# Column stage of a 2048-point transform: factorization 64 x 32 with stacked real and imaginary parts, one PSUM bank and one set of tasks per frequency

## Chip, cores and metric

One core of one Trainium2 chip. Its engines are PE (TensorE, matmuls), DVE (VectorE), ACT (ScalarE) and POOL (GpSimd); SPq is the queue of SyncE, which issues the transfers. An eviction is the copy of a matmul's result out of PSUM (`ps` in the profile lines). The metric is the device time of one launch in microseconds (us), as a median over several launches.

## The reference

```python
def reference(A_x, A_w_r, A_w_i, B_x, B_w_gate, B_w_up, B_w_down):   # all bf16
    x  = A_x                                    # [1, 2048, 640]
    xn = layernorm(x, axis=-1)
    X  = rfft2(xn, axes=(-2, -1)) * (A_w_r + 1j * A_w_i)             # weights [2048, 321]
    ya = irfft2(X, s=(2048, 640))
    yb = ((xn @ B_w_gate) * (xn @ B_w_up)) @ B_w_down                # 640 -> 1536 -> 640
    return x + ya + yb
```

There are two independent branches: a spectral filter and a gated feed-forward layer. The kernel interleaves them, so that the matmuls of one fill the waits of the other.

## The kernel before

The kernel is written as a list of tasks, each with the engines that it may run on, a duration, its reads and writes, and a priority. At build time a greedy planner places the tasks by these durations. That fixes the order of instructions on every engine; semaphore waits are then derived from the dependencies. The planner counts for a transfer:

```python
_DMA_LEAD = 500.0; _DMA_LAT = 1150.0; _DMA_ISSUE = 500.0     # ns
...
def hold(t, *later):        # t may not start before what `later` waits for is there
    for x in later:
        t.deps |= set(d for d in x.deps if d is not t and d not in later)
```

The 2048 rows are transformed as 64 (stage R, before) times 32 (column stage). The column stage runs in 16 steps. Each step holds two frequencies on two groups of 64 partitions, with the real and the imaginary parts in two PSUM banks:

```python
# for t in range(16):           filter rows: 4 transfers per step, four slots
def em_d(c, t=t):               # D: transform along the 640 axis
    for k in range(5):
        n = 128 if k < 4 else 130
        ins = c.e.matmul(psflat[:, bk*512 + k*128: ... + n], v_uq[:, k, t, :], v_fd[:, k*128: k*128 + n], ...)
# eD: two copies PSUM -> bf16 (128 x 512 and 128 x 130)
def em_c(c, t=t, ar=ar):        # C: complex product with the twiddled table, four matmuls
    c.e.matmul(ps[:, bk,     0:_LP], v_tf[:, t, 0, :], a_r, start=True,  stop=False)
    c.e.matmul(ps[:, bk + 1, 0:_LP], v_tf[:, t, 0, :], a_i, start=True,  stop=False)
    c.e.matmul(ps[:, bk,     0:_LP], v_tf[:, t, 1, :], a_i, start=False, stop=True)
    return c.e.matmul(ps[:, bk + 1, 0:_LP], v_tf[:, t, 2, :], a_r, start=False, stop=True)
# WM (DVE): four products of 256 and one of 260 elements with the filter, f32
# CD (DVE), CB (POOL): combine them to a complex product, bf16
# NG (ACT): three negated or copied pieces
def em_ia(c, t=t, ar=ar):       # IA: back along the rows, ten matmuls of 128 columns
    for k in range(5):
        c.e.matmul(dst, l1, v_ti[:, t, 0, :], start=True,  stop=False)
        ins = c.e.matmul(dst, l2, v_ti[:, t, 1, :], start=False, stop=True)
# eIA: one copy of 128 x 640
```

## Time and profile before

| | before |
|---|---|
| time, median of 3 runs | 206.84 us (206.67 to 207.27) |
| span of the profiled run | 204.3 us |
| PE / DVE / ACT / POOL busy | 98% / 87% / 59% / 11% |
| PE work of the column stage (D, C, IA) | 22.2 us |
| PE waits after 80 us | 0.35 us |

"PE work" counts every matmul by the distance from its start to the start of the next one, since a pipelined matmul is recorded with its latency. A "PE wait" is what is left of such a distance over 90 ns after the streaming time of the matmul is taken off (columns / 2.4 + 2.5 ns, which the spacings of 56, 136 and 216 ns for 128, 320 and 512 columns fit). A missing record of a 512-column matmul is put back first: only where the rest is a multiple of 216 ns, and only as many as the trace lacks of the 360. The profile lines are in the prediction below.

### The profile page before, as it was taken

The page shows a single profiled execution, that of the slowest core. Times are in us where ns is not written, and L with a number is a line of the kernel's source. Part 1 is how long each engine was busy: PE and PEld are TensorE (multiplying, and loading weights), DVE is VectorE, ACT ScalarE, POOL GpSimd, SP SyncE. Part 2 cuts the span into 40 slices and gives each one's busy share as a digit, 9 for nine tenths or more (in the row PEclk, how much of TensorE's full clock was granted, in tenths as well). Part 3 has the DMA queues.
Part 4 walks back from the last instruction along what each step waited for, and adds up shares of the span by engine and source line. Part 5 has one row for each costly group of instructions (what it writes and reads, how often), then busy time and mean ns, then how long its engine had stood idle before and what let it go on. Part 6 is the DMA issues. An engine that isn't in the chain of part 4 may idle for free.

```text
span 204.3 us, 4499 instructions
## 1 busy us (share of the span) xinstructions
PE 199.7 (98%) x1681; PEld 137.2 (67%) x1695; DVE 178.7 (87%) x508; ACT 121.4 (59%) x282; POOL 21.8 (11%) x36
## 2 busy tenths in 40 slices
PE   7999999999999999999999999999999999999995
PEld 7998999554545455465777666666777787777774
DVE  3798999999999999949997997818999999999973
ACT  2379998999976577577999899878420222000000
POOL 0000000000000000003655365310000000000000
PEclk9999999999999999999999999999999999999999
DMA  6999993603139460001333343225033122324212
GB/s 179 301 342 383 387 210 15 67 0 64 32 66 242 86 202 0 3 0 27 66 65 60 68 113 65 65 70 158 0 98 113 55 76 83 112 80 111 83 35 62
DMA packets 30740, 21.69 MB, mean 106 GB/s; under 512 B 10752, under 2 KB 29696, under 8 KB 30592
## 3 DMA queue, kind: packets, MB, share of 16 engines
q1 hardware_dynamic: 29920, 21.06, 40.6%
q10 hardware_dynamic: 800, 0.36, 0.6%
q8 instruction: 13, 0.21, 0.4%
q14 instruction: 7, 0.06, 0.1%
HBM read 16.82 MB, written 2.62 MB: 95 GB/s over the span
## 4 chain that ended last, share of the span: by engine, by line
PE 92%; DVE 6%; issue 1%; ACT 1%
PE ps L969 36%; PE ps L1229 26%; PE ps L989 13%; DVE arena L1070 3%; PE ps L747 3%; PE ps L930 2%; PE ps L1146 2%; PE ps L1239 2%; PE ps L1034 2%; PE ps L1117 2%; PE ps L1118 2%; DVE arena L1073 1%; PE ps L1058 1%; PE ps L1055 1%; PE ps L1057 1%; PE ps L1056 1%
## 5 line engine op out<-in xcount | busy, mean ns | idle before, releaser
L719 ACT ACTIVATE arena<-ps 128x512 bf16<-128x512 f32 (+5 forms) x183 | 97.1, 568 | 48.7 <-PE ps L1146 23.4
L969 PE MATMUL ps<-arena 128*128 128x512 bf16 x346 | 80.1, 379 | 0.9 <-DVE arena L1073 0.3
L969 PEld LDWEIGHTS ps<-arena 128*128 128x128 bf16 x360 | 33.9, 98 | 36.5 <-ACT arena L719 0.8
L1229 PE MATMUL ps<-arena 128*128 128x320 bf16 (+2 forms) x396 | 56.7, 295 | 0.0
L1229 PEld LDWEIGHTS ps<-arena 128*128 128x128 bf16 x396 | 38.0, 98 | 13.9
L989 PE MATMUL ps<-arena 128*128 128x128 bf16 (+1 forms) x360 | 28.2, 237 | 0.1
L989 PEld LDWEIGHTS ps<-arena 128*128 128x128 bf16 x360 | 24.9, 98 | 2.5 <-ACT arena L719 0.7
L1070 DVE TENSOR_TENSOR arena<-ps,arena 128x256 f32<-128x256 f32 x64 | 22.6, 414 | 1.4 <-PE ps L1058 1.2
L1005 DVE TENSOR_TENSOR arena<-arena 128x512 bf16<-128x512 bf16 x36 | 15.3, 425 | 9.0 <-ACT arena L719 8.8
L1093 POOL TENSOR_TENSOR arena<-arena 128x256 bf16<-128x256 f32 x16 | 10.3, 644 | 111.5 <-DVE arena L1086 111.5
L1249 DVE TENSOR_TENSOR arena<-ps,arena 128x320 bf16<-128x320 f32 (+2 forms) x33 | 15.3, 473 | 3.8 <-PE ps L1239 3.8
L1094 POOL TENSOR_TENSOR arena<-arena 128x256 bf16<-128x256 f32 x16 | 11.9, 745 | 0.0
L1117 PE MATMUL ps<-arena 128*128 128x128 bf16 x80 | 10.4, 219 | 0.1
L1118 PE MATMUL ps<-arena 128*128 128x128 bf16 x80 | 10.4, 219 | 0.0
L1117 PEld LDWEIGHTS ps<-arena 128*128 128x128 bf16 x80 | 8.7, 111 | 1.7
L1118 PEld LDWEIGHTS ps<-arena 128*128 128x128 bf16 x80 | 8.7, 112 | 1.4
L1239 PE MATMUL ps<-arena 128*128 128x320 bf16 (+2 forms) x33 | 9.1, 295 | 0.0
L883 DVE TENSOR_TENSOR arena<-arena 128x384 f32<-128x384 bf16 x16 | 8.8, 551 | 0.0
L773 ACT ACTIVATE arena<-arena 128x640 bf16<-128x640 bf16 x10 | 8.3, 825 | 0.0
L782 DVE BATCH_NORM_STATS2 arena<-arena 128x6 f32<-128x320 bf16 x12 | 5.4, 481 | 2.8 <-DMA arena<-in_A_x_dram 2.7
L767 ACT ACTIVATE arena<-arena 128x640 bf16<-128x640 bf16 x10 | 7.3, 734 | 0.3 <-DMA arena<-in_A_x_dram 0.2
L1073 DVE TENSOR_TENSOR arena<-ps,arena 128x260 f32<-128x260 f32 x16 | 7.0, 438 | 0.0
(72 smaller groups left out, 235.7 us busy)
## 6 DMA issues: line engine op xcount, KB each, us to landing
arena<-in_A_x_dram SPq DMA_DIRECT2D x20, 160.0 KB, 2.5
out_dram<-arena SPq DMA_DIRECT2D x31, 80.0 KB, 1.6
arena<-c_tf SPq DMA_DIRECT2D x4, 384.0 KB, 11.2
arena<-in_A_w_r_dram SPq DMA_DIRECT2D x32, 40.1 KB, 2.3
arena<-in_A_w_i_dram SPq DMA_DIRECT2D x32, 40.1 KB, 2.3
arena<-in_B_w_gate_dram SPq DMA_DIRECT2D x4, 320.0 KB, 5.4
arena<-in_A_x_dram SPq DMA_DIRECT2D x1, 1280.0 KB, 10.3
arena<-c_ti SPq DMA_DIRECT2D x2, 512.0 KB, 4.9
```

The costliest lines, as they stand in the source:

```text
L719: return c.e.activation(dst, src, _ACTF.Copy)
L969: ins = c.e.matmul(ps[:, bk, :], v_gw[:, w, j, ft, :], v_xt[:, j, rows], start=(j == 0), stop=(j == 4))
L989: ins = c.e.matmul(ps[:, bk, w * n:(w + 1) * n], v_gw[:, w, j, ft, :], v_xt[:, j, rows], start=(j == 0), stop=(j == 4))
L1005: return c.e.tensor_tensor(v_ht[:, ft0, rows], v_gbf[:, rr, 0, :], v_gbf[:, rr, 1, :], _OP.mult)
L1070: c.e.tensor_tensor(v_p[:, ar, w, :, 128 * h:128 * h + 128].rearrange("p c (m k) -> p c m k", k=4), xh.rearrange("p c (m k) -> p c m k", k ...
L1093: c.e.tensor_tensor(v_y[ar][:, 512:768], p01[:, 0:256], p10[:, 0:256], _OP.add)
L1094: return c.e.tensor_tensor(v_y[ar][:, 256:512], p00[:, 0:256], p11[:, 0:256], _OP.subtract)
L1117: c.e.matmul(dst, l1, v_ti[:, t, 0, :], start=True, stop=False)
L1118: ins = c.e.matmul(dst, l2, v_ti[:, t, 1, :], start=False, stop=True)
L1229: ins = c.e.matmul(ps[:, bk, 0:sl3.stop - sl3.start], v_ht[:, ft, a * 128:(a + 1) * 128], v_wd[:, ft, sl3], start=(ft == 7 and px is None) ...
L1239: return c.e.matmul(ps[:, bank_of(own), 0:sl3.stop - sl3.start], v_sm[:, 2, :], v_v[:, a, sl3], start=False, stop=True)
L1249: return c.e.tensor_tensor(v_out[:, a % 2, sl3], ps[:, bk, 0:sl3.stop - sl3.start], v_xr[:, xs, sl3], _OP.add)
```

## The change

The intent is to halve the C matmuls, since PE bounds the kernel, and to give every frequency its own small tasks. The factors become 32 (stage R) and 64 (column stage). Real and imaginary rows of one frequency lie on partitions 0-63 and 64-127, so one matmul with a [[re, im], [-im, re]] table does a whole complex product. In the same way IA's contraction adds up the products with the filter, and the combines (CD, CB) vanish. The main lines, shortened:

```diff
-_R = 32
+_R = 64
-_NW = 4
+_NW = 2                       # slots of filter rows ...
+_WQ = 4                       # ... each now holds four frequencies
 # filter rows: every second step, six transfers (two of 64 partitions from a
 # broadcast source, four of every other partition), with each row fetched twice
-            td = T("D_%d" % t, "pe", 5 * _d_mm(128), em_d, ... bank="pair", cls="a")
+            for w in range(2):           # w: real, imaginary
+                    for k in range(5):
+                        n = 64 if k < 4 else 65
+                        ins = c.e.matmul(ps[:, bk, k * 64:k * 64 + n], v_uq[:, k, t, :], ...)
+                def em_ed(c, td=td, ar=ar, w=w):
+                    for g in range(2):
+                        ins = copy_on(c, v_a[64 * w:64 * w + 64, ar, 324 * g:324 * g + 321],
+                                      ps[64 * g:64 * g + 64, bk, 0:321])
+            for g in range(2):           # one frequency q = 2t + g each
+                    return c.e.matmul(ps[:, bank_of(c.t), 0:_LP], v_tf[:, q, :], v_a[:, ar, 324*g:324*g + _LP], ...)
                 # WM (DVE): two products of 256 and one of 130 elements, written as bf16
+                wm = T("WM_%d" % q, "dve", 895.0, em_wm, reads=[(b_w, slot of the filter rows)], ..., frees=tc)
+                hold(tc, wm)             # so C waits for the filter rows as well
                 # NG: one negation of 256, on POOL, ACT or DVE
+                def em_ns(c, yr=yr, g=g):
+                    c.e.tensor_copy(yg[:, 833:896], yg[:, 1025:1088])
+                    c.e.tensor_copy(yg[:, 961:1024], yg[:, 769:832])
+                    return c.e.tensor_scalar(yg[:, 896:961], yg[:, 1024:1089], -1.0, None, _OP.mult)
+                T("NS_%d" % q, "pool", 700.0, em_ns, ...)
                 # IA: ten matmuls of 64 columns; eIA: one copy of 128 x 320
 # start: 10 groups of warm-up matmuls instead of 12, smaller fill matmuls, first
 #        statistics partly on ACT
 # schedule: other caps, priorities and slacks (retuned)
... (tables, buffers and views cut)
```

## The prediction

> **What bounds the kernel now.** I read the page first (busy shares, slices, chain), then the groups by form, then a table of windows, then single pieces of the chain.
>
> ```profile
> PE 199.7 (98%) x1681; PEld 137.2 (67%) x1695; DVE 178.7 (87%) x508; ACT 121.4 (59%) x282; POOL 21.8 (11%) x36
> ...
> PEclk9999999999999999999999999999999999999999
> ...
> PE 92%; DVE 6%; issue 1%; ACT 1%
> PE ps L969 36%; PE ps L1229 26%; PE ps L989 13%; DVE arena L1070 3%; PE ps L747 3%; PE ps L930 2%; PE ps L1146 2%; PE ps L1239 2%; PE ps L1034 2%; PE ps L1117 2%; PE ps L1118 2%; DVE arena L1073 1%; PE ps L1058 1%; PE ps L1055 1%; PE ps L1057 1%; PE ps L1056 1%
> ```
>
> TensorE (PE) is busy 98% of 204.3 us at full clock, and 92% of the chain that ended last is matmuls. A busy PE need not be at its peak, so I checked that with the spacing of matmuls in the chain: ten 128-column ones in 0.56 us (56 ns each), five 512-column ones in 1.08 us (216 ns), twelve 320-column ones in 1.63 us (136 ns). These are the array's streaming time plus about 2.5 ns, so nothing is left inside the groups either.
>
> The groups by form give the counts of the part that changes, the column stage (D = L1034, C = L1055 to L1058, IA = L1117 and L1118), and the vector work beside it:
>
> ```profile
> L1034 PE MATMUL ps<-arena 128*128 128x128 bf16 x64 | 5.9, 218 | 0.0
> L1058 PE MATMUL ps<-arena 128*128 128x321 bf16 x16 | 4.8, 300 | 0.0
> L1117 PE MATMUL ps<-arena 128*128 128x128 bf16 x80 | 10.4, 219 | 0.1
> L1117 PEld LDWEIGHTS ps<-arena 128*128 128x128 bf16 x80 | 8.7, 111 | 1.7
> L1034 PEld LDWEIGHTS ps<-arena 128*128 128x128 bf16 x80 | 5.6, 97 | 1.4
> L1070 DVE TENSOR_TENSOR arena<-ps,arena 128x256 f32<-128x256 f32 x64 | 22.6, 414 | 1.4 <-PE ps L1058 1.2
> L1094 POOL TENSOR_TENSOR arena<-arena 128x256 bf16<-128x256 f32 x16 | 11.9, 745 | 0.0
> ```
>
> The 219 ns is the latency of one pipelined matmul, not its cost; the cost is the spacing, 56 ns. The weight loads overlap the matmuls.
>
> Windows by stage (us, then PE, PEld, DVE, ACT, POOL busy, clock, DMA):
>
> ```profile
> 28.00:60.00 32.00, 31.84 (x245) 19.50 (x246) 31.17 (x97) 28.99 (x68) 0.00 (x0) 1.00 0.35 49
> 100.00:112.00 12.00, 11.95 (x123) 8.60 (x123) 10.57 (x37) 11.59 (x33) 6.65 (x10) 1.00 0.32 64
> 112.00:125.00 13.00, 12.62 (x115) 8.50 (x117) 12.51 (x42) 11.94 (x35) 6.93 (x10) 1.00 0.39 84
> 145.00:165.00 20.00, 20.00 (x171) 15.10 (x170) 19.63 (x49) 3.47 (x6) 0.00 (x0) 1.00 0.28 80
> ```
>
> In the column stage (about 89 to 137 us) PE stays full because gate/up matmuls (L969) are interleaved as filler, while VectorE (DVE) and ScalarE (ACT) are nearly full as well. So DVE and ACT are a close second there, and DVE is again in the inverse stage, 145 to 185 us.
>
> **The PE ledger.** With those spacings: L969 360 x 216 = 77.7; L989 240 x 56 + 120 x 109 = 26.5; L1229 52.2; L1239 4.4; L930 and L1146 160 x 56 = 8.9; transposes L844 1.1; column stage D 80 x 56 = 4.5, C 64 x 136 = 8.7, IA 160 x 56 = 8.9, together 22.1. Sum 192.9 us (counts from the program, since some records are missing). The other 11.4 us are: 6.1 before the first transpose (the warm-up matmuls L747, 48 of them in 5.30), 1.1 of cold transposes and fill matmuls before the first gate/up matmul at 7.57, some 1.7 of gaps, and 2.4 after the last matmul. A gain must therefore come out of PE work or out of the start; a wait removed elsewhere has at most 1.7 us to give.
>
> **What the Trainium skill says.** "TensorE: Matmul & The Clock Gate", section "Wait — 56ns, not 53.3ns?": spacing N/2.4 + about 2.5 ns when warm, and a floor of about 25 ns however small N is. The trace agrees for 128, 320 and 512 columns; no matmul of 64 columns is in it. The section "Weight-path perf modes — Fast Weight Load (FWL) and DoubleRow" of that page says that a full 128-column bf16 load is read in four parallel chunks. The trace fits: where PE had run dry (9.47 us), the load and its first matmul start within 0.01 us of each other and the second load starts about 15 ns after the first, so I estimate that a contiguous load holds the array for about 14 ns. IA's stride-4 loads take some 16 ns longer (111 ns mean of L1117, which mixes contiguous ones in, against 97 of L1034), so about 31 ns by estimate. "VectorE: DVE Perf Modes", section "Why PSUM operands drop a tier": fp32 from PSUM runs one element per cycle. The trace agrees (256 elements in 414 ns, four in a row at 330 ns each), so writing the products as bf16 makes none of them faster. "GPSIMD Engine Reference", section "4.1 Engine selection": two-input work is about 2x slower there than on VectorE, one-input roughly at line rate. L1094 at 745 ns agrees with the first; no one-input copy on POOL is in the trace.
>
> **The change part by part.**
>
> *C, removed PE work.* Real and imaginary rows are stacked on the contraction side, so a complex product of 128 rows that took four matmuls becomes two products of 64 frequencies-by-sign each in one matmul: 64 x 136 ns = 8.7 us become 32 x 136 = 4.4. **-4.4 us**, all on the bound engine.
>
> *D, more matmuls.* 80 of 128 columns become 160 of 64, each with the full 128-column weights again. At 64/2.4 + 2.5 = 29 ns, the contiguous load (14 ns) hides: 160 x 29 = 4.7 against 4.5. **+0.2.**
>
> *IA, more matmuls.* 160 of 128 columns become 320 of 64. Four fifths have stride-4 weights; the next load can start only when the previous matmul has started, so I take 33 ns for those (31 + about 2) and 29 for the rest: 256 x 33 + 64 x 29 = 10.3 against 8.9. **+1.4.**
>
> PE total of the column stage: 22.1 - 4.4 + 0.2 + 1.4 = 19.3, **-2.8 us**.
>
> *DVE.* Per old step it does 4 x 330 + 370 + two 65-element combines of about 140, together about 2.0 us, x16 = 32 us. After: per frequency two 256-element products and one of 130, about 330 + 330 + 220 = 0.88, x32 = 28 us. The combines vanish, because IA's contraction does the adding. About **-4 us of DVE**, off the path while PE is full.
>
> *ACT.* D's eviction must now move halves between partitions: four copies of 64 x 321 per step. Between 382 ns for 256 and 595 for 512 elements a 321-element copy costs about 436, so 1.75 us per step instead of 0.88 (595 + 283), +14 us in all. IA's eviction becomes 2 x 436 instead of 705, +2.7. The three negate/copy operations (412 + 247 + 246 = 0.9 per step, 14.5 us) move to POOL, or partly to ACT or DVE. ACT stays about even.
>
> *POOL.* From 21.8 us to perhaps 32 x (0.4 to 0.9 for the negation + 0.6 for three short ones) = 32 to 48 us, by estimate from the two-input rows above, in a stage of 48. Near full, but some of the negation may go elsewhere.
>
> *Weights.* The filter rows come in groups of four frequencies, double-buffered, twice the bytes (each row is fetched for its real and imaginary partition). A group is six transfers; before, two issues on the queue took 1.23 us, so six take about 3.7 us plus 2.3 to land, about 6 us, while the other group lasts some 48/8 = 6 us. Tight, but each may run ahead by a group.
>
> *Start.* 40 warm-up matmuls in place of 48: at 107 ns (48 weight loads in 5.04 us) that is 0.86 us less. The first normalised block is ready at 5.42 (L826 starts 5.03, lasts 0.39), the transposes start at 6.15, so at most about 0.7 can be had; early weight loads may take a part back. I count **-0.6**.
>
> *End.* The inverse stage and the output matmuls are the same work. Accumulators go from four banks to three and additions to the end get a late priority. I count 0, with a spread.
>
> Sum: 204.3 - 2.8 - 0.6 = 200.9 us of span; the timed run is 2.5 longer than the span now (206.84 against 204.3), so **203.4**. I take off 0.2 because the schedule has been retuned and POOL relieves a stage that had its few gaps there (0.38 of 13 us in 112:125): **203.2 us**, -1.8%.
>
> **Rivals.**
>
> *A, small matmuls cost only streaming time and the retuning pays.* IA at 29 ns gives another -1.0, the start gives -0.8, gaps shrink by 0.7. About 201.4 us, -2.6%. For it: the loads hidden everywhere in this trace, DVE relieved. Against it: the longer stride-4 loads, and gaps that are few already.
>
> *B, the weight path or the issue binds at 64 columns.* A pair of load and matmul may need 40 ns. Then D is 6.4 and IA 12.8, together 19.2 against 13.4, which eats C's saving: +1.4 instead of -2.8, about 207.5 us. At 56 ns it would be 27 against 13.4 and the kernel about 4% slower, 215 us. For it: no 64-column matmul has been seen here, and the number of PE pairs in the stage rises from 304 to 512. Against it: the 15 ns between two loads at 9.47.
>
> *C, another engine or a transfer becomes the bound of the column stage.* The chain of one frequency is D, eviction, C, product, negation on POOL, IA, eviction; POOL at 48 us or a late weight group would stall PE, since every engine's order is fixed at build time. PE can only be held up when the gate/up filler placed there is used up. 1 to 4 us lost, 204 to 207 us. For it: ACT and POOL near full. Against it: PE lost only 0.4 us where DVE and ACT were both over 90%.
>
> **Range and chances.** The centre is the sum above; A sets the low end, a mild B or C the high one: 200.8 to 206.8 in 8 of 10 cases. The 2% line lies at 202.7, only 0.5 below the centre, so faster 0.40, same 0.50; slower (over 211) needs B at its worst or C with a real stall: 0.10.
>
> **What would show it.** Right: spacing of the 64-column matmuls of 29 to 34 ns; one C matmul per frequency at 136 ns; PE still at 97% or more; the first transposes near 5.5 us; DVE and ACT below or at the old load. Wrong: 64-column spacing of 40 ns or more (B), PE gaps in the column stage put down to POOL or to filter transfers (C), or an inverse stage in which PE waits for VectorE because three accumulator banks are too few.

## The result

| | before | after |
|---|---|---|
| time, median (same rounds, 4 runs each) | 207.06 us (206.67 to 207.80) | 210.06 us (209.99 to 210.34) |
| ratio | | 1.0143, 95% interval 1.0111 to 1.0175 |
| span of the profiled run | 204.3 us | 207.9 us |
| PE work of the column stage | 22.2 us | 19.75 us |
| PE waits after 80 us | 0.35 us | 6.26 us |

A ratio is the mean time of one kernel's fast runs over that of the other's of the same rounds, so not quite the ratio of the medians. The output is correct. The change made the kernel 1.4% slower. That is inside the 2% class, but 6.9 us above the predicted 203.2 and above the range.

The page of the changed kernel (busy times, slices of PE, POOL, clock, and the chain that ended last):

```profile
PE 198.3 (95%) x1908; PEld 134.7 (65%) x1925; DVE 179.9 (87%) x513; ACT 129.8 (62%) x287; POOL 32.1 (15%) x108
...
PE   7899999999999999899989997997999999999995
...
POOL 0000000000000000193474566262000000000000
PEclk9999999999999999999999999999999999999999
...
PE 60%; DVE 24%; DMA 6%; SPq 4%; issue 3%; ACT 1%; POOL 1%; POOLq 0%
```

Before, PE had 98% and the chain was 92% PE. Now the chain goes through DVE for 24%, and through transfers and their issuing queue (SPq) for 10%. DVE has not lost the 4 us that I expected, and ACT has gained 8 and POOL 10.

**What went as predicted.** Groups of the changed kernel by form (busy, mean ns of one, idle before and its releasers):

```profile
L1052 PE MATMUL ps<-arena 128*128 128x64 bf16 x128 | 7.4, 193 | 0.0
L1126 PE MATMUL ps<-arena 128*128 128x64 bf16 x160 | 13.6, 197 | 0.3 <-POOL arena L1112 0.3
L1075 PE MATMUL ps<-arena 128*128 128x321 bf16 x32 | 7.5, 300 | 3.3 <-issue 1.7 <-DMA arena<-in_A_w_i_dram 1.0 <-DVE arena L716 0.5
L1090 DVE TENSOR_TENSOR arena<-ps,arena 128x256 bf16<-128x256 f32 x64 | 24.0, 416 | 1.0 <-PE ps L1075 0.8
L715 ACT ACTIVATE arena<-ps 64x321 bf16<-64x321 f32 x46 | 20.0, 434 | 2.9 <-PE ps L1052 2.2
L716 DVE CAST arena<-ps 64x321 bf16<-64x321 f32 x18 | 8.8, 490 | 0.5 <-PE ps L1052 0.3
```

The mean of one matmul is its latency; its cost is the spacing. From start to start, D (L1052) takes 29.6 ns x 160 = 4.74 us, C (L1075) 137.6 x 32 = 4.40, IA (L1126 and L1127) 33.2 x 320 = 10.61. That is 19.75 us against 22.2 before (4.46 + 8.78 + 8.93), so **-2.4 us** where I had -2.8. No other large group changed its spacing by more than 1 ns. At the start, the 20 transposes went from 70 to 57 ns, and the fill matmuls became smaller.

**What did not.** The third line shows a wait of 3.3 us in front of C. The chain of work that ended last has it in detail (start, length, what):

```profile
98.11 0.55 SPq L709
98.70 0.60 SPq L709
99.34 0.60 SPq L709
99.99 0.60 SPq L709
100.64 0.60 SPq L709
101.28 3.63 DMA arena<-in_A_w_i_dram
104.95 0.45 PE ps L1075 x2
```

Six issues of 0.6 us stand in a row on one queue (the sixth is the first part of the 3.63 us), the last transfer lands 3.0 us after its issue has ended, and C starts at once. The timeline of PE at that place (start, duration, in brackets the idle time before):

```profile
97.32 0.43 PE L1075 MATMUL ps<-arena 128*128 128x321 bf16 x2 [0.22 <-issue]
...
102.87 1.24 PE L974 MATMUL ps<-arena 128*128 128x512 bf16 x5
103.95 0.30 PE L1075 MATMUL ps<-arena 128*128 128x321 bf16 x1
104.95 0.45 PE L1075 MATMUL ps<-arena 128*128 128x321 bf16 x2 [0.70 <-DMA arena<-in_A_w_i_dram]
```

The C at 103.95 is the last of the group of filter rows that had landed; the next C needs the next group. The buffer for that group came free at 98.11, when the products (WM) of its last user were done, and the rows were there at 104.91: 6.8 us. The same happens at 97.32 (the rows landed at 97.23), at 118.99 and at 127.42. The four waits are 0.38, 0.87, 0.47 and 1.63 us, **3.35 us** in all. (When I wrote the expectations below I had counted three: I had taken the one at 97.32 in part for a missing record.) The planner had counted 0.5 us per issue and 1.9 us from the end of the last issue to its landing, 4.9 us for the group. In its plan the rows are there in time (building the kernel again shows every group landing at least 0.5 us before its first C), so it put no filler in front of these C.

The other waits of PE are one of 0.71 us in front of the first C (at 85.34 us, for the eviction on DVE), one of 0.31 at 93.78 (also for an eviction on DVE), and five at the end of the column stage. Timeline of PE, ACT and POOL there (lines between left out):

```profile
142.00 0.38 POOL L1112 TENSOR_SCALAR arena<-arena 128x65 bf16<-128x65 bf16 x1
...
142.52 0.20 PE L1126 MATMUL ps<-arena 128*128 128x64 bf16 x1 [0.26 <-POOL arena L1112]
...
142.83 0.19 PE L1127 MATMUL ps<-arena 128*128 128x64 bf16 x1
...
143.06 0.44 ACT L715 ACTIVATE arena<-ps 128x320 bf16<-128x320 f32 x1 [0.17 <-PE ps L1127]
...
143.64 2.28 PE L1155 MATMUL ps<-arena 128*128 128x128 bf16 x30 [0.62 <-ACT arena L715]
```

This is the last piece of a dependency chain: NS on POOL, IA, eviction, stage I (L1155), which needs all frequencies. PE has nothing else to do. In the kernel before, gate/up matmuls (L969) were still left there, before and after the first matmuls of stage I (L1146):

```profile
136.68 1.03 PE L969 MATMUL ps<-arena 128*128 128x512 bf16 x4
137.55 0.72 PE L1146 MATMUL ps<-arena 128*128 128x128 bf16 x10
138.10 1.24 PE L969 MATMUL ps<-arena 128*128 128x512 bf16 x5
```

From the first D to the first I the column stage took 48.4 us before (89.12 to 137.55) and takes 61.0 now (82.66 to 143.64). It has less PE work, lasts longer, and uses up more filler: of the 360 gate/up matmuls of 512 columns 120 stood in it before and 15 were left after it; now it is 165, and none is left. The retuned settings do not do this by themselves: b_both below (new settings, old stage) takes 49.8 us and 120 of them, three_slots (new settings, new stage, no filter waits) 57.7 us and 165. The waits at the end sum to 1.9 us (0.42 + 0.78 + 0.12 + 0.30 + 0.27). Unlike the filter waits, they stand in the plan already.

### The profile page after: what moved, and what is told of

Same layout as the page of the kernel before. It is cut to its first block, busy times and chain, and to the rows that moved or that the text cites. A ratio compares the mean times of both kernels' runs of the same rounds, so it can differ in the third digit from the quotient of the medians.

```text
span 207.9 us, 5045 instructions
## 1 busy us (share of the span) xinstructions
PE 198.3 (95%) x1908; PEld 134.7 (65%) x1925; DVE 179.9 (87%) x513; ACT 129.8 (62%) x287; POOL 32.1 (15%) x108
## 4 chain that ended last, share of the span: by engine, by line
PE 60%; DVE 24%; DMA 6%; SPq 4%; issue 3%; ACT 1%; POOL 1%; POOLq 0%
PE ps L1238 23%; PE ps L974 17%; PE ps L994 9%; SPq L709 4%; DMA arena<-in_A_w_i_dram 3%; DMA arena<-in_B_w_up_dram 3%; DVE arena L716 3%; DVE arena L1010 2%; PE ps L1248 2%; DVE arena L1090 2%; PE ps L1075 2%; PE ps L1126 2%; DVE arena L899 2%; PE ps L1155 2%; PE ps L1127 2%
## 5 line engine op out<-in xcount | busy, mean ns | idle before, releaser
L715 ACT ACTIVATE arena<-ps 128x512 bf16<-128x512 f32 (+6 forms) x214 | 106.3, 533 | 42.6 <-PE ps L1155 25.3
L974 PEld LDWEIGHTS ps<-arena 128*128 128x128 bf16 x360 | 33.2, 98 | 35.6 <-ACT arena L715 2.1
L1238 PE MATMUL ps<-arena 128*128 128x320 bf16 (+2 forms) x396 | 55.8, 295 | 0.0
L1238 PEld LDWEIGHTS ps<-arena 128*128 128x128 bf16 x396 | 37.9, 98 | 13.8
L1090 DVE TENSOR_TENSOR arena<-ps,arena 128x256 bf16<-128x256 f32 x64 | 24.0, 416 | 1.0 <-PE ps L1075 0.8
L1103 POOL TENSOR_SCALAR arena<-arena 128x256 bf16<-128x256 bf16 x8 | 6.8, 853 | 89.5 <-DVE arena L1093 89.5
L716 DVE CAST arena<-ps 64x321 bf16<-64x321 f32 (+1 forms) x25 | 12.2, 490 | 8.3 <-PE ps L1127 7.8
L1126 PEld LDWEIGHTS ps<-arena 128*128 128x128 bf16 x160 | 12.6, 116 | 3.1 <-issue 0.3
L1126 PE MATMUL ps<-arena 128*128 128x64 bf16 x160 | 13.6, 197 | 0.3 <-POOL arena L1112 0.3
L1127 PE MATMUL ps<-arena 128*128 128x64 bf16 x160 | 13.6, 198 | 0.0
L1127 PEld LDWEIGHTS ps<-arena 128*128 128x128 bf16 x160 | 11.5, 115 | 2.0
L1112 POOL TENSOR_SCALAR arena<-arena 128x65 bf16<-128x65 bf16 x32 | 12.0, 374 | 0.0
L1110 POOL COPY arena<-arena 128x63 bf16<-128x63 bf16 x32 | 8.7, 273 | 20.6 <-DVE arena L1093 20.3
L1075 PE MATMUL ps<-arena 128*128 128x321 bf16 x32 | 7.5, 300 | 3.3 <-issue 1.7
L1093 DVE TENSOR_TENSOR arena<-ps,arena 128x130 bf16<-128x130 f32 x32 | 9.3, 292 | 0.0
```

The lines of the kernel that those rows point to most:

```text
L715: return c.e.activation(dst, src, _ACTF.Copy)
L716: return c.e.tensor_copy(dst, src)
L974: ins = c.e.matmul(ps[:, bk, :], v_gw[:, w, j, ft, :], v_xt[:, j, rows], start=(j == 0), stop=(j == 4))
L1075: return c.e.matmul(ps[:, bank_of(c.t), 0:_LP], v_tf[:, q, :], v_a[:, ar, 324 * g:324 * g + _LP], start=True, stop=True)
L1090: c.e.tensor_tensor(dst, xh.unsqueeze(1).to_broadcast([128, 2, 32, 4]), wv, _OP.mult)
L1112: return c.e.tensor_scalar(yg[:, 896:961], yg[:, 1024:1089], -1.0, None, _OP.mult)
```

## The experiments

**Theory A**: the waits for filter rows cost about 3 us, because two slots of four frequencies, loaded by six issues, are too slow for the order that the planner fixed. **Rival B**: the transfers only happen to be last; ACT, DVE and POOL would hold PE at the same places. A later theory, **E**, is about the rest: with the filter waits gone the kernel would still only equal the one before, so the freed PE time has gone somewhere.

Several kernels are wrong, to take a cost away; this is said each time. "Orders kept" means that I compared the planned order of each engine with that of the parent kernel and found them identical (for the runs without some transfers: of the instructions that remain).

### three_slots: a third slot for filter rows, orders kept, correct

```diff
-_NW = 2
+_NW = 3     # the third slot lies in areas that are dead in this stage;
             # a load now also waits for the whole layernorm (addresses cut)
```

> The changed kernel with a third buffer for a group of four filter-row frequencies; the order of every compute engine is the same, the result stays right. Theory A (PE stands in its fixed order before the first product matmul of a group because the two-deep filter loads land too late: 0.87 us at 103.95, 0.47 at 118.4, 1.64 at 125.6 in the trace of after): these three waits vanish and the time falls by 2.5 to 3.2 us, to about 207.1. Theory B (the order itself is short of filler and another wait, POOL's short operations or an eviction, takes their place): less than 1 us falls, 209.3 or more.

Measured 207.15 us (206.70 to 208.12); before, in the same rounds, 206.89; ratio 1.002 (0.9985 to 1.0055); span 204.5. Theory A holds: the median is 2.9 us lower, and the span of the profiled run 3.3, which is the sum of the four waits. All other waits of PE in the stage are as they were. The group of C in this kernel (compare the third line of the groups above):

```profile
L1085 PE MATMUL ps<-arena 128*128 128x321 bf16 x32 | 7.0, 300 | 0.7 <-DVE arena L726 0.5
```

Both releasers for filter rows are gone from it.

### no_hold: C no longer waits for filter rows, VectorE alone does; orders kept, correct

```diff
-                hold(tc, wm)
+                tc.deps |= set(d for d in wm.deps if d is not tc and not d.nbytes)
```

> The changed kernel with two buffers, but the product matmul no longer waits for the filter rows, only VectorE's multiplication does; all orders the same, result right. Theory A: PE runs on into the gate/up matmuls behind the product, so a late load costs PE only what lies beyond that slack: 1 to 3 us fall, 207.2 to 209. If instead the load itself is the pace of the stage, so that it does not matter which engine waits, under 0.7 us falls.

Measured 207.02, ratio 0.9991 (0.9968 to 1.0015), span 204.6. C may start without its filter rows; VectorE waits for them instead and catches up. So PE was held by a wait that only VectorE needed. Late rows are harmless, then, if only VectorE waits for them.

### no_reload: only the first two groups of filter rows are loaded; orders kept, wrong

```diff
+        gone = set(t for t in sch.tasks if <load of a later group>)
+        sch.order["sp"] = [t for t in sch.order["sp"] if t not in gone]     # and from all deps
```

> Wrong result on purpose: filter rows are loaded for the first two groups alone and read again by all the others; compute orders the same, 36 of 50 filter transfers gone. The bound of what the filter transfers can cost. Theory A: the same 2.5 to 3.2 us as with a third buffer, about 207.1. If the bytes or the issue queue cost something beyond the waits, it comes out clearly lower than the third buffer; theory B: 209.3 or more.

Relative error 0.035, as intended. Measured 206.77, ratio 0.999 (0.9965 to 1.0016). With no such transfers at all the gain is again about 3 us. So about 3 us is the whole cost of the filter rows, and a third slot already gets it all.

### ns_tail: the three short pieces (NS) of the last two frequencies on VectorE; PE's order kept, correct

```diff
-                T("NS_%d" % q, "pool", 700.0, em_ns,
+                T("NS_%d" % q, "dve" if q >= 30 else "pool", 520.0 if q >= 30 else 700.0, em_ns,
```

> The changed kernel with the short mirror operations of the last two frequencies on VectorE in place of POOL; PE's order the same, result right. After the last product matmul PE waits 0.42 us at 142.07 and 0.78 at 142.83 before the inverse stage may start. If POOL's chain of three short operations (about 0.8 us per frequency) sets that, 0.4 to 0.9 us falls (209.2 to 209.7); if the eviction of the last inverse product and the empty filler set it, under 0.3.

Measured 210.55, ratio 1.0171 (1.0142 to 1.0200). The wait of 0.42 us for POOL shrank to 0.15, but the 0.78 us for the last eviction stayed, and the filter waits were 0.79, 0.74, 0.80 and 1.97, 1.0 us more in sum than in the changed kernel. So the time says little here (the plan also moved one negation from DVE to ACT); by the trace, the last POOL pieces cost at most the 0.27 us that went.

### b_start: the kernel before with the change's start alone, correct

```diff
-        nwarm = opts.get("nwarm", 12)
+        nwarm = opts.get("nwarm", 10)
... (smaller fill matmuls, first statistics partly on ACT)
```

> The kernel before with the change's start alone: 40 warm-up matmuls in place of 48, fill matmuls of 64 columns only after the first transposes, statistics of block 1 on ScalarE. If the start is worth what the prediction counted (0.6 us), about 206.3 beside 206.9 of before; if the first gate/up matmuls meet their weights' arrival instead, so that a part of it is given back at once, within 0.3 us of before.

Measured 207.06 against 207.02, ratio 0.9998 (0.9967 to 1.0028). The start is worth nothing. In the changed kernel the first gate/up matmul does start 0.38 us earlier (7.19 against 7.57), and then PE waits 0.40 us at 8.52 for gate/up weights that have not landed. In b_start itself it starts at 7.13 and then waits 0.79 us for the same weights. The 0.6 us that I counted were limited by a transfer.

### b_both: the kernel before with the start and the retuned schedule, old column stage, correct

```diff
+        sch.caps = {"glu": 3, "acc": 3, "fill": 1}        # were 2, 4
+        iv_prio 19, fin_prio 41, i_rate 0.05, slacks 700/800/2000, affinity 600   # were 30, 5, 0.2, 500/600/1500, 300
... (and three more of this kind)
```

> The kernel before with the change's start and its retuned schedule (caps on PSUM banks, priorities, slacks), the old column stage kept. If the retuning is good in itself, 205.5 to 206.5. If it only fits the new column stage, the same or up to 1.5 us slower than before (the build-time plan of this kernel is 1.0 us longer than that of before).

Measured 207.64, ratio 1.0022 (0.9994 to 1.0050). The retuned settings do not help by themselves. PE waits after 80 us are 1.89 us in this run.

### a_oldtune: the changed kernel with the old settings of the schedule, correct

```diff
-        caps, priorities and slacks of the change
+        caps, priorities and slacks of the kernel before
```

> Correct. The changed kernel with the schedule settings of the kernel before. My prediction counted the retuning of the schedule as worth 0.2 us. If that is right, 210.0 to 210.6. If the new column stage needs a schedule of its own (because its work on ACT, DVE and POOL is larger and finer), 212 to 216.

Measured 218.97 (218.20 to 219.74), ratio 1.0566; the clock of the profiled run was 0.992. That is above even the larger expectation. PE waits after 80 us are 13.4 us, not counting a stretch at half clock (0.52 from 96 to 99 us). So the new settings are no bonus; the new column stage needs them.

### plan_all: two slots, but the planner is told the measured durations, correct

```diff
+        if name.startswith("ld_w") and name[4] != "d": t.dur = {"sp": 645.0}     # an issue; 500 before
+        # and 600 ns more to landing; evictions, POOL pieces and IA as measured
-                T("NS_%d" % q, "pool", 700.0, em_ns,
+                T("NS_%d" % q, "pool", 880.0, em_ns,
```

> Correct. Two slots as in the changed kernel, with the build-time plan told the durations that the trace shows (a filter issue 645 ns and a landing 600 ns later, IA 33.2 ns, the evictions, POOL's products), and the orders that come of that. If the three waits for filter rows come from a plan that took the transfers to be shorter than they are, the waits go even with two slots: 207 to 208.7. If two slots are too few in whatever order, it stays at 209.5 or more.

Measured 207.48 (206.74 to 207.88), ratio 1.0014 (0.9985 to 1.0043). Within the first expectation. With two slots and the `hold` as they were, the order alone gives 2.6 us back (a wait of 0.16 us for filter rows is left). So the waits needed three things together: a group that lands late, a C that waits for it, and an order made for **durations counted too short**. Taking any one away is enough. That it was the transfers' durations, and not those of the evictions, POOL or IA, is likely, since C waits for a landing, but this run changed all of them at once.

At this point A is settled in four ways, and the kernel stands at about 207.0, where the kernel before stands. PE has 2.4 us less to do, and gains nothing. The next runs look for them.

### three_keep2: three slots, the last two gate/up groups held back until the last IA is issued, correct

```diff
+        for g_ in gu4s[-2:]:
+            g_.deps.add(ia)
```

> Three filter buffers, and the last two gate/up matmul groups held back until the last inverse product of the column stage has been issued. Theory D (the 2 us of PE waits at the end of the column stage come from filler used too early): the waits are filled and the time falls by 1 to 2 us from three_slots, to about 205.5. Rival (the stage is paced by evictions and by ScalarE, VectorE and POOL, so filler taken away from one place leaves a hole there): the time is the same as three_slots or up to 2 us longer, 207 to 209.

Measured 209.74 (208.89 to 211.17), ratio 1.0130 (1.0076 to 1.0185). Two of its four runs had a granted clock of 0.992 (210.39 and 211.17); the two at 1.0 took 208.89 and 209.08, still slower than before. The waits moved and grew: 1.98 us between C and IA at 136.39, 0.60 at 138.80 and 1.33 at 148.91. So the filler was not merely used too early: where these two groups are taken away, PE has to wait for the other engines.

### three_half_best: each pair of 64 x 321 evictions halved to one 128 x 321, settings searched again, wrong on purpose

```diff
-                    for g in range(2):
-                        ins = copy_on(c, v_a[64*w:64*w+64, ar, 324*g:324*g+321], ps[64*g:64*g+64, bk, 0:321])
-                    return ins
+                    return copy_on(c, v_a[:, ar, 324 * w:324 * w + 321], ps[:, bk, 0:321])
```

> Wrong result on purpose: three filter buffers, and each eviction of the row products D is one copy of 128 x 321 in place of two of 64 x 321, so some 14 us of ScalarE and VectorE work are gone; PE's work is the same (schedule settings chosen anew for it). Theory E (ScalarE and VectorE, loaded by the doubled evictions, set the pace at which PE can leave the column stage with filler in hand): 1 to 3 us below three_slots, 204 to 206. Rival (only the dependency chain at the end counts): within 0.7 us of three_slots.

Relative error 0.0285, as intended. Measured 205.97 (205.64 to 206.70), ratio 0.9936 (0.9903 to 0.9969). The waits at the stage's end are gone except one of 0.40 us, but a wait of 1.08 at 93.55 is new. This speaks for E, and not for much.

### three_half_fixed: the same halving, orders kept, wrong

(The same edit, with the planned durations left as they were.)

> Wrong on purpose (the imaginary parts of the transformed input are left out of the store, so the output is off by a few per cent). It is the three-slot kernel with each frequency's two evictions of 64x321 halved to one copy of 128x321, with the order of every engine kept exactly as in the three-slot kernel. Theory E (the column stage is paced by the sum of ACT, DVE and POOL work, but at orders that are fixed at build PE is already full while filler lasts, so that work taken from the evictions shows only where PE waits for an eviction directly): only the 0.49 us wait of the first column product shrinks, 0 to 0.6 us below the three-slot kernel, 206.5 to 207.2. Rival (the evictions themselves hold PE through the stage): 1.5 us or more below it, under 205.7.

Measured 205.68 (205.49 to 205.96), ratio 0.9933 (0.9912 to 0.9953), span 203.8. This **missed** my expectation of 206.5 to 207.2 and just met the rival's. The trace shows less than the times do: of the waits after 80 us the 0.71 in front of the first C is gone, and the 0.31 and the five at the end are unchanged (2.91 to 2.21 us).

### three_best: three slots, settings searched again, nothing else, correct

```diff
+           opts={'slack_act': 900, 'cap_glu': 2, 'cap_glu2': 1, 'i_rate': 0.2, 'f_prio': 6.05})
```

> Correct. Three slots for the filter rows, and the settings of the schedule searched again for that kernel. If the end-of-stage waits are only a matter of the order, a re-search alone should take them away and the kernel should come to 204.5 to 205.5. If they come from the amount of ACT, DVE and POOL work, a re-search alone gives little: 206.0 to 207.2, and the gain of the halved run belongs to the halving. It is also the candidate to beat the kernel before.

Measured 206.83 (206.67 to 207.46), ratio 0.9993 (0.9968 to 1.0017). A search of the settings alone does not move the waits at the end: they are the same five, 2.91 us with the 0.70 and 0.31 ahead of them.

### three_slots_b: three_slots once more, as reference for the next two

> The three-slot kernel once more, unchanged, as the reference of the next two on their chip: its four runs before scattered from 206.7 to 208.12. If the 1.5 us between it and the halved kernel at the same orders was partly scatter between chips and runs, it comes to 206.4 to 206.8 here; if not, to 207.0 to 207.4.

Measured 207.06 against 207.02, ratio 0.9998 (0.9967 to 1.0029). So the halved kernel's gain of some 1.3 us is real in the times, though its waits after 80 us explain only 0.7 of it.

### lean_fixed: halved evictions, and of NS's three pieces one alone after the first eight frequencies; orders kept, wrong

```diff
+                    if q < 8:      # keeps all of the buffer initialised
                         c.e.tensor_copy(yg[:, 961:1024], yg[:, 769:832])
                         c.e.tensor_scalar(yg[:, 896:961], yg[:, 1024:1089], -1.0, None, _OP.mult)
                     return c.e.tensor_copy(yg[:, 833:896], yg[:, 1025:1088])
```

> Wrong on purpose: the three-slot kernel with evictions halved and, after the first eight frequencies, one of POOL's three pieces of NS alone, all orders kept. Theory: at fixed orders, PE waits at the end of the column stage for the latency of the last evictions (0.78 and 0.43 us) and for POOL (0.42 us); only POOL's can go. 205.2 to 205.8, that is 0 to 0.4 us below the halved kernel. Rival (POOL's amount of work holds PE in the whole stage): 1 us or more below the halved kernel, under 204.7.

Measured 205.74 (205.69 to 206.07), ratio 0.9937 (0.9907 to 0.9968). At kept orders, POOL's work beyond its last piece costs nothing that the time shows (205.74 against 205.68). The wait for POOL (0.42) is gone; that for the last eviction is 0.93. The waits at the end belong to the order and its lack of filler.

### lean_best: the same cuts, settings searched again and more widely, wrong

```diff
+           opts={'slack_act': 900, 'slack_dve': 1200, 'cap_glu': 3, 'cap_glu2': 1, 'c_rate': 2.6, 'i_rate': 0.05,
+                 'iv_prio': 19.0, 'fin_prio': 5.0, 'ln_prio': 5.99, 'ng_eng': ('act', 'dve')})
```

> Wrong on purpose: the same cuts in ACT, DVE and POOL work as in the run with fixed orders, with the schedule searched again for them. Theory E (the PE time freed in the column stage was turned into waits at its end because that stage has more ACT, DVE and POOL work): with that work cut and the schedule free to use it, PE's 2.4 us come out whole, 203.8 to 205.0. Rival (the waits at the end are there whatever the other engines' work, as the new stage leaves PE less work to put beside it): 205.6 to 206.5, as in both halved runs.

Measured **203.21** (203.09 to 203.29), ratio 0.981 (0.9775 to 0.9845), span 201.2. That is a little below the expected 203.8 to 205.0. The page and PE's timeline at the end of its column stage (L984 is gate/up, L1163 stage I):

```profile
PE 196.6 (98%) x1908; PEld 135.4 (67%) x1925; DVE 170.9 (85%) x494; ACT 123.6 (61%) x282; POOL 13.6 (7%) x52
```

```profile
133.44 0.72 PE L1163 MATMUL ps<-arena 128*128 128x128 bf16 x10
134.22 1.03 PE L984 MATMUL ps<-arena 128*128 128x512 bf16 x4
135.08 0.72 PE L1163 MATMUL ps<-arena 128*128 128x128 bf16 x10
135.64 2.32 PE L984 MATMUL ps<-arena 128*128 128x512 bf16 x10
137.80 0.72 PE L1163 MATMUL ps<-arena 128*128 128x128 bf16 x10
```

Gate/up matmuls are left over for the change to stage I, as in the kernel before, and PE waits 0.25 us after 80 us. Here PE's shorter column stage comes out whole: the span is 3.0 us below the 204.3 of the kernel before, 2.4 for the stage and 0.5 for a first gate/up matmul at 7.10 in place of 7.57. (The medians differ by 3.8 us, as most runs of the kernel before are longer than its profiled one.) It is one plan out of many, so a rival is that its settings, or the width of the search, made it and not the cuts. No run tests that. The planner can be asked without a run, though: it reckons 203.2 us for lean_best, and 210.4 for three_slots with the settings of lean_best. So by its reckoning the settings are no gain without the cuts.

### half_wide and nons_wide: one of the two cuts each, searched as widely, wrong

> Wrong on purpose: three slots, evictions of the transformed input halved, POOL's three pieces kept, the schedule searched as widely as for the run that came to 203.21. The cut there was of two things at once. If the evictions (ACT and VectorE) were what mattered: 203.2 to 204.5. If POOL's pieces were: 205.5 or more, no better than the halved kernel at fixed orders. If both must go: in between.

Evictions halved, NS whole: measured 205.71 (205.24 to 206.65), ratio 0.9931 (0.9889 to 0.9972). PE waits after 80 us 1.63. That is the branch "if POOL's pieces were" of the expectation, no better than the halved kernel at fixed orders.

> Wrong on purpose: three slots, evictions whole, one of POOL's three pieces alone after the first eight frequencies, the schedule searched as widely. If POOL's pieces were what mattered: 203.2 to 204.5. If the evictions were: 206.0 to 207.1, no better than the three-slot kernel. If both must go: in between, 204.5 to 206.0.

NS cut, evictions whole: measured 208.05 (208.01 to 208.81), ratio 1.0037 (1.0001 to 1.0074). PE waits after 80 us 4.39. This lies above every branch of the expectation. It was badly chosen: the best plan had put every negation (256 elements, 869 ns) on POOL, which rose to 37.9 us, where lean_best has none there. So the run says nothing clear of POOL's share. Halving the evictions alone gets a part and no more. How the rest splits between the engines, and how much of it is the luck of a plan, stays **open**.

### The waits of PE side by side

After 80 us, in the profiled runs:

| kernel | us, median | PE waits | of these: filter rows |
|---|---|---|---|
| before | 206.84 | 0.35 | 0 |
| after | 210.06 | 6.26 | 3.35 |
| three_slots | 207.15 | 2.91 | 0 |
| plan_all | 207.48 | 3.12 | 0.16 |
| half_wide (wrong) | 205.71 | 1.63 | 0 |
| lean_best (wrong) | 203.21 | 0.25 | 0 |

No correct version beat the kernel before: the lowest median is that of three_best, with 206.83 against 206.90 in its rounds, the same within the interval.

## Why the prediction was wrong, step by step

Measured in spans, it said 204.3 - 2.8 - 0.6 = 200.9, and 207.9 came: 7.0 us more. The terms:

| term of the sum | predicted | measured | by |
|---|---|---|---|
| C | -4.4 | -4.38 | spacing, 64 to 32 matmuls |
| D | +0.2 | +0.28 | spacing |
| IA | +1.4 | +1.68 | spacing, 33.2 ns mean |
| start | -0.6 | 0 | b_start |
| waits for filter rows | 0 | +3.35 | trace; about 3 in three_slots, no_hold, no_reload |
| other PE waits of the stage and its end | 0 | +2.56 | trace: 6.26 - 3.35 - 0.35 |

The differences sum to 0.4 + 0.6 + 3.35 + 2.56 = 6.9 of 7.0 us. (The trace of the changed kernel has 343 of the 360 gate/up matmuls of 512 columns, and 17 gaps of exactly one of them; every other gap is a wait.)

**Right.** PE's arithmetic: the spacings of 64-column matmuls were put at 29 and 29 to 33 ns and are 29.6 and 33.2, so Rival B was wrong. The durations of evictions (436 expected, 434 measured on ACT) and the rate of the products were right too.

**The step that failed first** is the one on *Weights*: "about 6 us, while the other group lasts some 6 us. Tight, but each may run ahead by a group." Its size was right (5.9 to 7.6 us measured for the six groups loaded again). The conclusion was wrong. A load can't run ahead here: with two slots, it starts only when the last product of the group two back is done. And PE's order is fixed by a plan that believed in 4.9 us, so there is no filler where the rows come late. I had written in Rival C that a late weight group would stall PE since orders are fixed, and then gave it little weight: it put 1 to 4 us on such stalls, and 3.35 + 2.56 came. "PE can only be held up when the gate/up filler placed there is used up" was the false sentence: PE is held up wherever the *next instruction in its order* waits, however much filler stands behind it. The `hold` line puts VectorE's need for filter rows on PE, which no_hold shows.

**The second** is "About -4 us of DVE, off the path while PE is full", with "ACT stays about even". The evictions and negations that the prediction lists had to run somewhere. By busy times of the groups, ACT's own work in the stage did stay even (38 us before, 37 after; that ACT as a whole went from 121.4 to 129.8 comes from statistics, normalisations and copies outside the stage). DVE's did not fall by 4 but rose by 9 (38.7 to 47.5): products and combines gave back 3.4, while 18 of the 64 new evictions (490 ns, 8.8 us), seven of IA's and eight negations came. POOL went from 21.8 to 32.1, the low end of its estimate. "Off the path while PE is full" was the false part: the stage became longer (57.7 us without filter waits against 49.8 with the same settings and the old stage), and a longer column stage consumes filler that PE then lacks at the stage's end. Freed PE time became waits of 2.6 us. three_keep2 shows that holding two groups of filler back does not mend it, three_best that another search of the settings does not, and lean_best that with less of that work PE's gain comes out whole, in one plan. Which of the three engines holds the stage is not shown.

**The third** is small: 0.6 us for the start, limited by the landing of gate/up weights, and 0.2 for the retuning, which is no gain (b_both) but a need (a_oldtune).

## What to carry to other kernels

Where the order of every engine is fixed at build, a wait costs the engine that stands in front of it, with no regard to how much other work is queued behind. So ask of each new transfer whether the plan's time for it is the measured one, and which engine really needs the data. A saving on the full engine can be worth nothing, as here, if the stage it sits in is paced by the others: sum up *their* work in that stage too, and check whether enough filler is left when the stage ends.

## What the Trainium skill lacked or had wrong

- "TensorE: Matmul & The Clock Gate", section "Back-to-back issue gap", gives a sustained spacing of about 81 ns for 128 columns and about 131 ns for 512 in streams of weight load and matmul. Here 160 such pairs of IA before ran at 55.8 ns, and the 512-column gate/up matmuls at 216 ns. What the section calls the isolated gap is what held in the stream.
- The same section's table puts 1 to 64 columns at about 25 ns. With new weights for each, 64 columns took 29.6 ns (contiguous weights, D) and 33.2 ns in the mean of IA, four fifths of whose weights have stride 4. No page gives a figure for weight loads of such a stride.
- "GPSIMD Engine Reference", section "4.1 Engine selection", calls one-input work there roughly line rate. Here a negation of 256 bf16 elements took 853 ns on POOL, 416 on ACT and 247 on DVE; a copy of 63 took 271 ns on POOL (the profile's spans on POOL are rough).
- "SBUF — State Buffer", section "The DMA setup-cost knee", puts the setup of a transfer at some 50 ns plus a few hundred, and gives no figure for how long an issue holds its queue. Here each issue of filter rows held it for about 0.6 us, so six made 3.8 of the 6.8 us until the group was there.
- No page says outright that a copy from PSUM of half the partitions saves nothing: 64 x 321 took 434 ns on ACT and 490 on DVE, 128 x 321 took 443 and 489.
